# Chunked attention and a GELU layer: where the reciprocals of the first two tiles are spread, and which queue loads V

## The chip, the cores and the metric

The kernel runs on one core of a Trainium2 chip. The metric is the device time of one execution in microseconds (us); before the change it is 291.14 us, the median of three runs (290.89 to 291.3).

## The reference, cut to what matters

```python
B, H, S, D = 8, 8, 576, 64            # q, k, v: float32
q_c = q.reshape(B, H, 9, 64, D)       # chunks of 64 queries, of 64 keys
scores = np.matmul(q_c, k_c.transpose(0, 1, 2, 4, 3)) / np.sqrt(D)
attn = np.exp(scores - scores.max(-1, keepdims=True))
attn = attn / (attn.sum(-1, keepdims=True) + 1e-09)
x = np.matmul(attn, v_c)              # -> 4608 tokens x 512 (heads side by side)
h = x @ w_in                          # 512 -> 2048
y = gelu(h) @ w_out                   # 2048 -> 512, exact GELU; float32 out
```

Each chunk of 64 tokens attends to itself alone, so the softmax is over 64 keys. The kernel leaves the maximum out (the scores are small) and divides after the product with V: x = (P V) times the reciprocal of P's sums.

## The kernel before

**Tiles.** The 4608 tokens are cut into nine tiles of 512. Tiles 0 to 7 are the first eight chunks of one batch; tile 8 holds the ninth chunk of all eight batches. For each tile, attention makes x (128 partitions of model dimension x 4 groups `g` x 512 tokens; a group is a pair of heads), `mm1` makes h (16 slices `f` of 128 hidden units, four products of 128x128 with 128x512 each, then a GELU on ScalarE), and `mm2` makes y (four blocks `ms` of 128 tokens, sixteen products each). TensorE's products are bf16 into float32 PSUM banks.

**PSUM.** Eight banks: three of the tag "mm", two "tp", three "at". A tile that asks for a bank of a tag waits until one is free.

**Order.** The whole program is written out by hand (`manual_schedule`): every engine works through its instructions in the order in which the program issues them. While a tile's `mm1` and `mm2` run (`phase`), the attention of the next tile is put between the products: `extra2` names what goes ahead of which step of `mm2`. SyncE's queue (SP) issues nearly all transfers, in order.

**The first tile** has nothing to hide behind. For each group: cast q (VectorE) and k (POOL), transpose them on TensorE (`att_T`, copied out by VectorE for q and ScalarE for k), scores (`att_S`), exp on ScalarE, then `att_av`: P's columns are the stationary operand and V with a column of ones (`v_one`) moves, so that av lies with queries on partitions and its 65th column holds the sums. VectorE takes the reciprocals (line 329) and multiplies (line 331; for one half of group 2 ScalarE does so, line 335), `att_x` transposes the result back on TensorE (line 340) and a copy puts it into x (line 341). `keep_warm` puts products without use between these, and `mm1_first` starts the first two f group by group, as x comes (line 360). From f = 2 on, `mm1_slot` follows (line 371).

**The second tile's attention** lies inside tile 0's `mm2`, which runs by rows there: step s takes f = s for all four ms (`mm2_rows`, line 447), so that w_out is needed only as it arrives. At steps 3 to 8 q and k are transposed, at 9 the scores come (`quad_S`), at 11 the column sums by products with ones (`column_sums`, line 216), a 32x32-block transpose and a reciprocal on VectorE (lines 220, 222). `over` then moves the reciprocals between partitions with 16 small ScalarE copies (line 227), `spread` makes four 128x512 tiles of them by broadcasting transposes (line 231). At 12 come the product with V (`quad_av`, line 275) and the multiplication into x (`quad_x`, line 283). After steps 0 to 13, `mm2_last` adds the last two f to each ms (line 429), `rows_out` copies y out, and `mm1_first(1, ...)` makes four f of tile 1. Only then `phase(1)` goes on with line 371. Later tiles get their reciprocals in another way (`quad_total`, `quad_rc`), which stays.

**Loads.** SP issues, in order: q, k, V of tile 0 mixed with w_in's four quarters; then w_out's first quarter, tile 1's q, w_out's second, tile 1's k, w_out's third, tile 1's V (nine transfers of rows of 256 bytes, `rows_128` at line 105: four for even heads, five for odd ones), w_out's last quarter in two halves, and tile 2's q and k. All go through seven staging buffers of 1 MB and are cast to bf16 by POOL, VectorE or (one slice of w_out) ScalarE.

Of the kernel before, what the change touches and what calls it, by code (L numbers as in the profile page):

```python
# [11 lines left out]
def kernel(  # L12
# [9 lines left out]
    nc = tc.nc  # L22
# [28 lines left out]
    v_one = consts.tile([P, H, CT // 2, D + 2], bf16, name="v_one")  # L51
    nc.gpsimd.memset(v_one[:, :, :, D:D + 1], 1.0)
# [49 lines left out]
    def rows_128(t, src, raw, swapped, parity=range(2)):  # L102

        def go(to, rows):
            nc.sync.dma_start(to, rows.rearrange("h key d -> key h d"))
        last = CT // 2 - 1
        if t < B and not swapped:
            for n in range(CT // 2):
                go(raw[:, :, n], src[t, :, P * n:P * (n + 1), :])
        elif t < B and 0 in parity:  # L110
            for n in range(CT // 2):
                go(raw[:, 0::2, n], src[t, 0::2, P * n:P * (n + 1), :])
# [16 lines left out]
    def load_v_rows(t, parity=range(2)):  # L129
        if "vf" not in tiles[t]:  # L130
            tiles[t]["vf"] = stage_tile()[:].rearrange("p (h n d) -> p h n d", h=H, d=D)
        rows_128(t, v, tiles[t]["vf"], True, parity)

    def load_v(t, heads):

        if "vf" not in tiles[t]:
            tiles[t]["vf"] = stage_tile()[:].rearrange("p (h n d) -> p h n d", h=H, d=D)
        for h in heads:
            nc.sync.dma_start(tiles[t]["vf"][:, h], v[t, h, 0:MT, :].rearrange("(n key) d -> key n d", key=P))
# [8 lines left out]
    def cast_v(t, g, copy):  # L148
        copy(v_one[:, 2 * g:2 * g + 2, :, 0:D], tiles[t]["vf"][:, 2 * g:2 * g + 2])
# [62 lines left out]
    def column_sums(t):  # L212
# [10 lines left out]
        rb = work.tile([P, G, NB], f32, tag="rb1", name="rb1", bufs=1)  # L223

        def over(m):
            for s in range(G):
                nc.scalar.copy(rb[QD * s:QD * (s + 1), m], r1[QD * m:QD * (m + 1), s // 2])  # L227

        def spread(m):
            rc = work.tile([P, NB, 32], f32, tag="rc", name="rc", bufs=4)  # L230
            nc.vector.transpose(rc[:], rb[:, m].to_broadcast([P, NB, 32]))
            tiles[t]["rc", m] = rc
        return over, spread
# [79 lines left out]
    def att_av(t, g, banks, second=None):  # L313
# [3 lines left out]
        av = [pool.tile([P, half, D + 1], f32, tag=tag, name="av_ps") for pool, tag in banks]  # L317
        for n in range(half):
            for r in range(2):
                for c in range(2):  # L320
                    cs = slice(CH * c, CH * (c + 1))
                    nc.tensor.matmul(av[r][cs, n, :], st["pT", 2 * (g // 2) + r][cs, half * (g % 2) + n, :],
                                     v_one[cs, 2 * g + r, n, 0:D + 1], start=True, stop=True,
                                     tile_position=(CH * c, CH * c))
        xn = work.tile([P, half, 2, D], bf16, tag="xn", name="xn", bufs=4)
        st["xn", g] = xn
        rr = work.tile([P, 2, half, 1], f32, tag="rr", name="rr", bufs=4)
        for r in range(2):
            nc.vector.reciprocal(rr[:, r], av[r][:, :, D:D + 1])
            if r == 0 or second is None:  # L330
                nc.vector.tensor_tensor(xn[:, :, r], av[r][:, :, 0:D], rr[:, r].to_broadcast([P, half, D]),
                                        op=mybir.AluOpType.mult)
            else:
                for n in range(half):
                    nc.scalar.activation(xn[:, n, r], av[r][:, n, 0:D], Act.Copy, scale=rr[:, r, n])

    def att_x(t, g, copy, pool, tag):
        tp = pool.tile([P, CT // 2, P], bf16, tag=tag, name="tp")
        for n in range(CT // 2):
            nc.tensor.transpose(tp[:, n], tiles[t]["xn", g][:, n].rearrange("p r d -> p (r d)"), ident[:])  # L340
# [332 lines left out]
```

## Time and profile before

| | |
|---|---|
| median of the runs | 291.14 us (290.89 to 291.3) |
| the profiled execution | 290.1 us |
| its span (first to last instruction) | 288.3 us |
| TensorE busy | 277.9 us, 96% |
| ScalarE, VectorE, POOL busy | 60%, 36%, 25% |
| granted TensorE clock | full |
| moved by DMA | 53.87 MB, 187 GB/s over the span |
| end of the first attention (first `mm1_slot`) | 20.43 us |
| column sums of tile 1 | 44.66 us |
| first `mm1_slot` of tile 1 | 55.62 us |

All of it is one profiled execution, times counted from the span's start. A line such as L371 is a line of the kernel. Each row names the engine (PE is TensorE, DVE VectorE, ACT ScalarE, SP SyncE), the operation, its output and inputs by the program's names and the shape. Rows of the timeline join instructions that follow one another closely; matmuls overlap, so a group's time includes the tail of its last one. What stands in brackets is how long the engine had been idle before the row, and what ended that.

### The profile page before, as it was taken

How to read it: one execution, taken by the hardware profiler on the slowest of the kernel's cores; microseconds unless marked ns; L12 is line 12 of the kernel's file. 1: busy time of each engine (PE TensorE's matmuls, PEld its weight loads, DVE VectorE, ACT ScalarE, POOL GpSimd, SP SyncE). 2: the span in 40 equal slices, each digit the busy share in tenths (PEclk: the TensorE clock that was granted, in tenths of full speed). 3: DMA queues.
4: the chain of work that ended last, by engine and by line, in shares of the span. 5: the costliest groups of instructions: out<-in, count | busy, mean ns of one | idle time of the engine just before them, and what ended most of it. 6: DMA issues, size and time to landing. Idle time of an engine off the chain costs nothing.

```text
span 288.3 us, 5998 instructions
## 1 busy us (share of the span) xinstructions
PE 277.9 (96%) x2427; PEld 132.2 (46%) x2427; DVE 104.5 (36%) x201; ACT 174.2 (60%) x364; POOL 72.4 (25%) x121
## 2 busy tenths in 40 slices
PE   7689997999999999999999999999999999999994
PEld 3344453444444444444444444444444444444443
DVE  2744235304910391039202920293029301940021
ACT  3567749677646873777367736863786368637400
POOL 3545673611620620052015200620024110000000
PEclk9999999999999999999999999999999999999999
DMA  7999989799899926991699159834995590030033
GB/s 230 307 372 382 400 215 342 170 267 246 201 278 279 221 81 187 270 219 55 178 287 210 58 165 265 199 103 151 190 159 117 156 217 2 19 129 0 0 75 73
DMA packets 118939, 53.87 MB, mean 187 GB/s; under 512 B 97792, under 2 KB 111360, under 8 KB 118912
## 3 DMA queue, kind: packets, MB, share of 16 engines
q1 hardware_dynamic: 118752, 53.36, 70.8%
q8 instruction: 19, 0.31, 0.5%
q10 hardware_dynamic: 160, 0.13, 0.2%
q14 instruction: 8, 0.07, 0.1%
HBM read 36.70 MB, written 9.44 MB: 160 GB/s over the span
## 4 chain that ended last, share of the span: by engine, by line
PE 93%; ACT 2%; DVE 2%; DMA 1%; issue 0%; POOL 0%; SPq 0%; POOLq 0%
PE h_ps L371 41%; PE y_ps L386 38%; PE y_ps L447 3%; PE h_ps L360 2%; PE av_ps L275 2%; PE s_ps L196 2%; PE tp L155 1%; PE y_ps L415 1%; ACT rb L227 1%; DMA arrival<-in_k_dram 1%; PE warm L505 1%; PE y_ps L429 1%; ACT x L341 1%; PE tp L340 0%; DVE qT L157 0%; DVE q_nat L146 0%
## 5 line engine op out<-in xcount | busy, mean ns | idle before, releaser
L371 PE MATMUL h_ps<-x,w_in_sb 128*128 128x512 bf16 x552 | 120.6, 379 | 0.0
L373 ACT ACTIVATE h<-h_ps 128x512 bf16<-128x512 f32 x138 | 82.3, 598 | 60.1 <-PE h_ps L371 60.1
L386 PE MATMUL y_ps<-w_out_sb,h 128*128 128x512 bf16 x496 | 109.7, 379 | 0.0
L371 PEld LDWEIGHTS <-w_in_sb 128*128 128x128 bf16 x552 | 54.0, 98 | 65.2
L386 PEld LDWEIGHTS <-h 128*128 128x128 bf16 x496 | 47.4, 98 | 55.8
L241 DVE STREAM_TRANSPOSE pt<-pT 128x256 f32<-128x256 f32 x28 | 12.2, 437 | 110.4 <-ACT pT L207 110.4
L146 POOL CAST q_nat<-arrival 128x512 bf16<-128x512 f32 x31 | 18.0, 621 | 97.1 <-DMA arrival<-in_q_dram 94.6
L169 POOL CAST v_nat<-arrival 128x1024 bf16<-128x1024 f32 (+1 forms) x18 | 16.8, 945 | 40.3 <-DMA arrival<-in_v_dram 40.3
L510 ACT ACT_TABLE_LOAD x18 | 23.1, 1283 | 1.0 <-PEq L657 0.7
L254 ACT COPY part<-part 32x32 f32<-32x32 f32 x56 | 12.2, 219 | 15.1 <-DVE part L244 14.6
L287 DVE TENSOR_TENSOR x<-av_ps,rc 128x512 bf16<-128x512 f32 x28 | 18.9, 676 | 2.2
L244 DVE TENSOR_REDUCE part<-pt 128x16 f32<-128x512 bf16 x28 | 19.2, 686 | 1.0
L400 DVE COPY y_sb<-y_ps 128x512 f32<-128x512 f32 x10 | 6.9, 692 | 34.8 <-PE y_ps L386 34.8
L144 POOL CAST k_nat<-arrival 128x512 bf16<-128x512 f32 x28 | 16.2, 614 | 0.9 <-DMA arrival<-in_k_dram 0.9
L400 ACT COPY y_sb<-y_ps 128x512 f32<-128x512 f32 x25 | 14.2, 583 | 1.5 <-PE y_ps L429 0.7
L447 PE MATMUL y_ps<-w_out_sb,h 128*128 128x512 bf16 x56 | 13.6, 379 | 1.4 <-POOL w_out_sb L494 1.4
L207 ACT ACTIVATE pT<-s_ps 128x512 bf16<-128x512 f32 x28 | 14.3, 594 | 0.0
L505 PE MATMUL warm<-rest 128*128 128x512 bf16 x23 | 8.5, 460 | 1.7 <-DVE rest L47 1.2
L268 DVE STREAM_TRANSPOSE rc<-rb 128x512 f32<-128x512 f32 x14 | 9.9, 707 | 0.2
L268 DVE STREAM_TRANSPOSE rc<-across 128x512 f32<-128x512 f32 x14 | 9.8, 700 | 0.0
L494 POOL CAST w_out_sb<-arrival 128x512 bf16<-128x512 f32 x11 | 7.3, 693 | 6.2 <-DMA arrival<-in_moe_w_out_dram 6.1
L484 POOL CAST w_in_sb<-arrival 128x512 bf16<-128x512 f32 x10 | 6.8, 702 | 5.7 <-DMA arrival<-in_moe_w_in_dram 5.7
(66 smaller groups left out, 137.9 us busy)
## 6 DMA issues: line engine op xcount, KB each, us to landing
out_dram<-y_sb SPq DMA_DIRECT2D x32, 256.0 KB, 2.1
arrival<-in_v_dram SPq DMA_DIRECT2D x57, 128.0 KB, 3.9
arrival<-in_k_dram SPq DMA_DIRECT2D x28, 256.0 KB, 6.0
arrival<-in_q_dram SPq DMA_DIRECT2D x7, 1024.0 KB, 6.6
arrival<-in_moe_w_out_dram SPq DMA_DIRECT2D x3, 1024.0 KB, 12.8
arrival<-in_moe_w_in_dram SPq DMA_DIRECT2D x4, 512.0 KB, 5.5
arrival<-in_moe_w_in_dram SPq DMA_DIRECT2D x2, 1024.0 KB, 8.7
arrival<-in_v_dram SPq DMA_DIRECT2D x30, 64.0 KB, 2.6
```

Of the source, the lines that this page charges most:

```text
L144: copy(st[nm][:, :, g], st[nm + "f"][:, :, g].rearrange("p (q r) d -> p q r d", r=2))
L146: copy(st[nm][:, g].rearrange("p j r d -> p r j d"), st[nm + "f"][:, 2 * g:2 * g + 2])
L169: copy(st["v"][:, r::2, ns], st["vf"][:, r::2, ns])
L244: nc.vector.tensor_reduce(st["part", g2][:, c, :, :, 0], pt[:].rearrange("p n e u -> p n u e"), axis=mybir.AxisListType.X, op=mybir.AluOpT ...
L268: nc.vector.transpose(rc[:], tiles[t]["rb", g2][c].to_broadcast([P, NB, 32]))
L287: nc.vector.tensor_tensor(x.rearrange("p n (e u) -> p n e u", u=2), st["av"][g2][c][:].rearrange("p n (e u) -> p n e u", u=2), st["rc", 2 ...
L371: nc.tensor.matmul(h_ps[:], w_in_sb[:, ks, f * P:(f + 1) * P], st["x"][:, ks, :], start=(ks == 0), stop=(ks == KS - 1))
L373: nc.scalar.activation(st["h"][:, f, :], h_ps[:], Act.Gelu)
L386: nc.tensor.matmul(y_ps[:], st["h"][:, f, ms * P:(ms + 1) * P], w_out_sb[:, f, :], start=(f == 0), stop=(f == FF - 1))
L400: (AC if t == 0 or ms < 3 and t + 1 < NT else DV)(y_sb[:], y_ps[:])
L447: nc.tensor.matmul(tiles[t]["y_ps", ms][:], tiles[t]["h"][:, fi, ms * P:(ms + 1) * P], w_out_sb[:, fi, :], start=(fi == 0), stop=False)
L510: nc.scalar.activation(act_scratch[:, 0:1], rest[:, 0:1], func)
```

## The change

For the first tile, the sums no longer come with the product. `att_sums` makes them on TensorE from P and a matrix of two columns of ones and takes their reciprocals; `att_spread` multiplies these, each repeated over 64 columns, with a float32 matrix of ones and zeros (`ident_f`), so that the reciprocals of a pair of heads come out along the free dimension on all partitions, and ScalarE copies the bank to SBUF. `att_av` now has V as the stationary operand and P moving: d lies on partitions, as x needs it, and VectorE's multiplication writes x itself. `att_x` and `v_one` are gone.

For the second tile, `over` does its moves as eight float32 products of `ident_f` with the reciprocals, into a bank of the tag "at", from which the four transposes read. The last two f of tile 0's `mm2` (`mm2_last`) stand inside `mm1_first(1, ...)`, which makes two f instead of four.

V's even heads for tile 1 are issued from ScalarE's queue, one transfer each ahead of f = 4, 6, 8 and 10 of tile 0's `mm1`; its odd heads stay on SP. POOL casts the first piece of V between slices of w_out. The fourth slice of w_in's first quarter is cast by VectorE instead of POOL.

```diff
-    v_one = consts.tile([P, H, CT // 2, D + 2], bf16, name="v_one")
-    nc.gpsimd.memset(v_one[:, :, :, D:D + 1], 1.0)
+    ident_f = consts.tile([P, G, 2, QD], f32, name="ident_f")
+    for r in range(2):
+        nc.gpsimd.tensor_copy(ident_f[:, :, r], ident[:].rearrange("p (g e) -> p g e", e=QD))
+    ones_r = consts.tile([P, 64], bf16, name="ones_r")
+    nc.gpsimd.memset(ones_r[:], 0.0)
+    for c in range(2):
+        nc.gpsimd.memset(ones_r[CH * c:CH * (c + 1), c:c + 1], 1.0)
...
-        rb = work.tile([P, G, NB], f32, tag="rb1", name="rb1", bufs=1)
-        def over(m):
-            for s in range(G):
-                nc.scalar.copy(rb[QD * s:QD * (s + 1), m], r1[QD * m:QD * (m + 1), s // 2])
-        def spread(m):
-            rc = work.tile([P, NB, 32], f32, tag="rc", name="rc", bufs=4)
-            nc.vector.transpose(rc[:], rb[:, m].to_broadcast([P, NB, 32]))
-            tiles[t]["rc", m] = rc
+        def over():
+            rb = ps_at.tile([P, G, NB], f32, tag="at", name="rb_ps")
+            for m in range(G):
+                for r in range(2):
+                    nc.tensor.matmul(rb[CH * r:CH * (r + 1), m], ident_f[:, m].rearrange("p r e -> p (r e)"), r1[:, r],
+                                     start=True, stop=True, tile_position=(0, CH * r))
+            for m in range(G):
+                rc = work.tile([P, NB, 32], f32, tag="rc", name="rc", bufs=4)
+                nc.vector.transpose(rc[:], rb[:, m].to_broadcast([P, NB, 32]))
+                tiles[t]["rc", m] = rc
...
+    def att_sums(t, g, pool, tag):
+        st = tiles[t]
+        half = CT // 2
+        sT = pool.tile([P, half // 2, 2, 2], f32, tag=tag, name="sT")
+        for a in range(half // 2):
+            for r in range(2):
+                u = half * (g % 2) + 2 * a
+                nc.tensor.matmul(sT[:, a, r], st["pT", 2 * (g // 2) + r][:, u:u + 2].rearrange("p u e -> p (u e)"),
+                                 ones_r[:, 0:2], start=True, stop=True)
+        st["rr", g] = work.tile([P, half // 2, 2, 2], f32, tag="rr", name="rr", bufs=4)
+        nc.vector.reciprocal(st["rr", g][:], sT[:])
+
+    def att_spread(t, g, pool, tag):
+        st = tiles[t]
+        half = CT // 2
+        rc_ps = pool.tile([P, half, 2, CH], f32, tag=tag, name="rc_ps")
+        for a in range(half // 2):
+            for c in range(2):
+                for r in range(2):
+                    nc.tensor.matmul(rc_ps[CH * r:CH * (r + 1), 2 * a:2 * a + 2, c],
+                                     st["rr", g][:, a, r, c:c + 1].to_broadcast([P, D]), ident_f[:, :, 0],
+                                     start=True, stop=True, tile_position=(0, CH * r))
+        st["rc", g] = work.tile([P, half, 2, CH], f32, tag="rc", name="rc", bufs=4)
+        nc.scalar.copy(st["rc", g][:], rc_ps[:])
+
+    def att_av(t, g, banks):
+        st = tiles[t]
+        half = CT // 2
+        av = [pool.tile([P, half, CH], f32, tag=tag, name="av_ps") for pool, tag in banks]
         for n in range(half):
             for r in range(2):
                 for c in range(2):
-                    cs = slice(CH * c, CH * (c + 1))
-                    nc.tensor.matmul(av[r][cs, n, :], st["pT", 2 * (g // 2) + r][cs, half * (g % 2) + n, :],
-                                     v_one[cs, 2 * g + r, n, 0:D + 1], start=True, stop=True,
-                                     tile_position=(CH * c, CH * c))
...
+                    cs, rs = slice(CH * c, CH * (c + 1)), slice(CH * r, CH * (r + 1))
+                    nc.tensor.matmul(av[c][rs, n], st["v"][cs, 2 * g + r, n],
+                                     st["pT", 2 * (g // 2) + r][cs, half * (g % 2) + n, :], start=True, stop=True,
+                                     tile_position=(CH * c, CH * r))
+        x = st["x"][:, g, :].rearrange("p (n c e) -> p n c e", c=2, e=CH)
+        for c in range(2):
+            nc.vector.tensor_tensor(x[:, :, c], av[c][:], st["rc", g][:, :, c], op=mybir.AluOpType.mult)
...
-        keep_warm(1)
+        att_sums(0, 0, *at)
         att_T(0, "q", 2, DV)
         att_S(0, (1,))
-        keep_warm(1)
+        att_spread(0, 0, *mm)
         cast_qk(0, "q", 3, DV)
         att_T(0, "k", 2, AC)
+        att_sums(0, 1, *at)
         att_T(0, "q", 3, DV)
-        keep_warm(1)
         att_S(0, (2,))
+        att_spread(0, 1, *mm)
         att_T(0, "k", 3, AC)
         keep_warm(1)
         att_av(0, 0, (tp, tp))
+        att_sums(0, 2, *at)
         att_S(0, (3,))
         att_av(0, 1, (at, mm))
+        att_spread(0, 2, *mm)
         keep_warm(1)
-        att_x(0, 0, AC, *mm)
-        keep_warm(2)
-        mm1_first(0, (mm, mm),
...
+        mm1_first(0, (mm, tp),
+                  (((0, 1), (0,)), lambda: att_sums(0, 3, *at), lambda: keep_warm(1), lambda: att_av(0, 2, (at, at)),
+                   ((0, 1), (1,)), lambda: att_spread(0, 3, *mm), lambda: act_table(Act.Gelu), lambda: keep_warm(1),
+                   lambda: att_av(0, 3, (at, tp)), ((0, 1), (2,)), lambda: win[0](3, DV), lambda: keep_warm(1),
                    ((0, 1), (3,))))
+        v_arrival(1)
...
-                    load_v_rows(1)
+                    load_v_rows(1, (1,))
...
+        def late_casts():
+            a, b = slice(0, 2), slice(2, 4)
+            wout[2](0, PO)
+            wout[2](1, PO)
+            cast_v_rows(1, 0, PO, a)
+            wout[2](2, PO)
+            wout[2](3, PO)
+            cast_v_rows(1, 0, PO, b)
+            cast_v_rows(1, 1, PO, a)
+            cast_v_rows(1, 1, PO, b)
+            for i in (0, 1, 3):
+                wout[3](i, PO)
...
-                  12: [lambda: quad_av(1)]
+                  11: [lambda: over.append(column_sums(1))],
+                  12: [lambda: over[0](), lambda: quad_av(1)]
                       + [lambda m=m: quad_x(1, m // 2, m % 2) for m in range(G)] + [lambda: wout[3](2, AC)]},
-              by_rows=True, first=2)
+              by_rows=True, first=2,
+              extra1={**{4 + 2 * n: [lambda n=n: load_v_rows(1, (0,), (n,), nc.scalar)] for n in range(CT // 2)},
+                      12: [late_casts]})
         pool_cast_qk(2)
-        mm1_first(1, (mm, mm, tp, at),
-                  (((0, 1), (0, 1)), lambda: rows_out(0, 2), ((2, 3), (0, 1)), lambda: rows_out(0, 3),
-                   ((0, 1, 2, 3), (2, 3))))
+        mm1_first(1, (tp, at), (((0, 1), (0, 1)), *[lambda ms=ms: mm2_last(0, ms) for ms in range(MT // P)],
+                                ((0, 1), (2, 3))))
...
-            phase(t, e2, first=4 if t == 1 else 0)
+            phase(t, e2, first=2 if t == 1 else 0)
```

## The prediction

> **What bounds the kernel now.** The page's head and the chain that ended last come first: TensorE is the bound, 93% of the chain, so anything that delays it by 1 us costs 1 us unless it was waiting there anyway.
>
> ```profile
> span 288.3 us, 5998 instructions
> ...
> PE 277.9 (96%) x2427; PEld 132.2 (46%) x2427; DVE 104.5 (36%) x201; ACT 174.2 (60%) x364; POOL 72.4 (25%) x121
> ...
> PE 93%; ACT 2%; DVE 2%; DMA 1%; issue 0%; POOL 0%; SPq 0%; POOLq 0%
> ```
>
> From 55.6 us on, the chain is TensorE alone, 29.2 us a tile, and the change ends there. So I read TensorE's timeline up to that point (start, duration, line, idle before). A duration holds about 0.17 us of tail; what an operation costs in a row is start to start.
>
> ```profile
> 8.64 0.40 PE L155 MATMUL tp<-ident,q_nat 128*128 128x128 bf16 x4 [1.09 <-DVE q_nat L146]
> ...
> 20.00 0.59 PE L360 MATMUL h_ps<-x,w_in_sb 128*128 128x512 bf16 x2
> 20.43 12.25 PE L371 MATMUL h_ps<-x,w_in_sb 128*128 128x512 bf16 x56
> ...
> 41.20 1.03 PE L447 MATMUL y_ps<-w_out_sb,h 128*128 128x512 bf16 x4
> ...
> 44.66 0.48 PE L216 MATMUL sums_ps<-pT,ones_c 128*32 128x512 bf16 x4
> 45.08 1.04 PE L447 MATMUL y_ps<-w_out_sb,h 128*128 128x512 bf16 x4
> 46.05 0.74 PE L275 MATMUL av_ps<-pT,v_nat 64*64 64x64 bf16 x64
> 48.21 1.89 PE L447 MATMUL y_ps<-w_out_sb,h 128*128 128x512 bf16 x8 [1.43 <-POOL w_out_sb L494]
> 50.45 1.89 PE L429 MATMUL y_ps<-w_out_sb,h 128*128 128x512 bf16 x8 [0.35 <-ACT w_out_sb L494]
> 52.17 3.62 PE L360 MATMUL h_ps<-x,w_in_sb 128*128 128x512 bf16 x16
> 55.62 10.52 PE L371 MATMUL h_ps<-x,w_in_sb 128*128 128x512 bf16 x48
> ```
>
> Three marks: the head (first attention) ends at 20.43; the second tile's column sums start at 44.66, call it T; that tile's first four f end at 55.62. Between T and 55.62 TensorE waits 1.78 us, for the last quarter of w_out, which VectorE's and POOL's timelines set beside the chain of the reciprocals:
>
> ```profile
> 45.18 0.72 DVE L220 STREAM_TRANSPOSE t<-sums_ps 128x512 f32<-128x512 f32 x1 [3.02 <-PE sums_ps L216]
> 45.93 0.35 DVE L222 RECIPROCAL r<-t 128x32 f32<-128x32 f32 x1
> ...
> 38.64 2.29 POOL L494 CAST w_out_sb<-arrival 128x512 bf16<-128x512 f32 x4 [0.99 <-DMA arrival<-in_moe_w_out_dram]
> ...
> 47.55 1.86 POOL L494 CAST w_out_sb<-arrival 128x512 bf16<-128x512 f32 x3 [2.80 <-DMA arrival<-in_moe_w_out_dram]
> ```
>
> Last the stretches of two us (busy times, clock, share of the DMA engines, GB/s): the loads are saturated from 2 to 38 us, and only while V's 256-byte rows come is there slack.
>
> ```profile
> 28.00:30.00 2.00, 2.00 (x11) 0.93 (x10) 1.17 (x2) 1.32 (x3) 1.61 (x2) 1.00 1.09 400
> ...
> 40.00:42.00 2.00, 2.00 (x18) 1.03 (x14) 1.22 (x2) 1.04 (x2) 2.00 (x5) 1.00 0.72 161
> ...
> 58.00:60.00 2.00, 2.00 (x11) 0.94 (x10) 0.00 (x0) 1.42 (x3) 0.00 (x0) 1.00 1.03 232
> ```
>
> The profiled execution took 290.1 us, 1.8 outside its span; the median is 291.14, so I add differences to the median. About 0.2% (0.58 us) is what a measurement of this kernel tells from no change.
>
> **Part 1, the head.** Out go, per pair of heads, four transposes (0.22 us of TensorE), ScalarE's copy of x (0.58), one of two reciprocals (0.18). In come `att_sums` (4 products, a reciprocal of 0.18) and `att_spread` (8 float32 products, then a ScalarE copy of a 128x512 bank, 0.58). V's products are as before, and VectorE's two multiplications (0.42 and, behind it, 0.34) now write x. Nothing differs until q's third cast ends and TensorE resumes, 8.62. From there TensorE's list, at start-to-start prices: 4 groups of transposes at 0.24, 3 of scores and 4 of V at 0.25, 3 of sums at 0.24 (four weight loads, as for transposes), 5 warming products at 0.22, 4 pairs of h at 0.43: 6.25 us. Call one spread X. Three waits follow spreads, whatever X: the third scores need k's copy, queued on ScalarE behind the spread's copy (0.17 tail + 0.04 + 0.49 + 0.58 + 0.04 = 1.32, against 0.72 of TensorE's work: 0.60); the fourth the same (against 0.95: 0.37); the last h needs copy and two multiplications (0.17 + 0.04 + 0.58 + 0.04 + 0.76 + 0.04 = 1.63 against 1.12: 0.51). End of the head: 8.62 + 6.25 + 1.48 + 4X = 16.35 + 4X; it is at 20.43 now, so X = 1.02 breaks even. V's last cast (15.90) and w_in's casts are earlier than their uses then.
>
> X is in no row: no float32 product runs now. Low end: 128 columns at the bf16 price of a transpose (0.055), both column halves at once: 8 x 0.055 / 2 = 0.22. High end: a float32 product made of four parts (two bf16-sized halves of each operand), so as long as 512 bf16 columns (0.216), plus a weight load of 0.098 that nothing covers: 8 x 0.314 = 2.5. The nearest row is L216: four 512-column products on four column strips took 0.42 start to start where singly they would take 0.86, so two ran at a time. With such a pairing X is 0.86, without it 1.73; I take the middle, 1.3. Head: 21.55, 1.1 us later.
>
> In the trace 64-column weight loads take 107 ns, 128-column ones 98 (L322, L371). The Trainium skill, "TensorE: Matmul & The Clock Gate", section "Weight-path perf modes", has a rule against this part behind that: float32 weights, and loads of fewer than 128 columns, get no fast weight load. By its section "LDWEIGHTS" a 64-column load is an estimated 53 ns; uncovered, eight in each of four spreads would add 1.7 us, and the total would be 295.1 instead of 293.4. No float32 row shows it, and the sum leaves it out.
>
> POOL's new work before its first cast (two copies, three memsets for one removed, some 1 us by its 0.1 to 0.3 us rows) fits in its 2.64 us of idle there; without that cover k's first cast would be late by as much. w_in's fourth slice goes from POOL to VectorE (0.6 us), in time for f = 3. The warming products left out give their places to real ones.
>
> **Part 2, half of V.** Its nine transfers stay nine, but four leave SP, where they stood ahead of w_out's last quarter, for ScalarE's queue, 2 to 7 us after the head: into the saturated stretch. At 232 GB/s (the row at 58) 0.52 MB delays what follows by 2.3 us. w_out's third quarter lands at 38.6, is cast by 39.25 and used at 41.20: slack 1.95, so T cannot come much earlier than now however fast the head; a head 1.1 us later hides it all. In return w_out's last quarter is issued behind five V transfers, not nine, and lands 1 to 3 us earlier (1 MB at 360 to 400 GB/s behind half the rows): the 1.78 us of waits go. V takes its staging buffer first, and each later load gets the buffer freed next; the fourth of w_out keeps that of w_in's fourth, cast by 26.4. POOL casts V's first piece between w_out's slices: +0.6 us for the third of these, used over 1 us later.
> Each issue also holds ScalarE's queue. SP's V issues took 0.50 to 2.03 us, median 0.61. A GELU takes 0.60 of each 0.86 us; two and a median issue make 1.81 against 1.73, a lag that three h banks absorb: 0. At 2.03 the lag is 1.5 each, 6.0 less 0.96 of slack: 5.0. I take 0, since its queue carries no other transfer, and keep 5.0.
>
> **Part 3, the second tile.** Out go 16 ScalarE copies (3.44 us, L227), in come 8 small float32 products (Y) into a third "at" bank; the four transposes of 0.71 stay. Reciprocals are there at T + 1.62; TensorE, done with its four products at T + 1.39, waits 0.27 with its own latency, then Y. Y: 64 products of V take 0.67, so at least 8 x 0.0105 = 0.08; at most eight loads of 0.107, 0.86; I take the middle, 0.45. Add 0.17: transposes start at T + 2.3 and take 3 x 0.63 + 0.71 = 2.6, to T + 4.9. The three "at" banks hold y's last rows, the sums and these products; V's second half needs the third, so TensorE stands from about T + 2.4 to T + 4.94. Behind the stop in its queue: 32 V products (0.34), 8 of w_out (1.73), then two f over half of x (0.86), eight closing w_out (1.73), the rest of the two f (0.86), two more f (1.73): T + 12.2. x's first half is multiplied by T + 6.2, no limit. Now it is T + 10.96: the 1.78 us of waits removed return as 2.8, plus Y, less 0.2 of tails that two stops fewer leave out. Cost: 1.2 us (0.9 with Y at its low end, 1.8 at its high end with transposes at 0.71).
>
> Sum: 1.1 + 0 + 1.2 = 2.3; 291.14 + 2.3 = 293.4.
>
> **Rivals.**
> A, cheap float32 (ends faster). If X is 0.5, the head ends 2.1 us earlier. For it speaks that nothing in the profile excludes it; against it L216 and the DMA share above 1.0. It decides only if the V half costs w_out less than it seems: with Y at its low end, faster by 0.58 needs T earlier by 1.5, so X at 0.65 or less and w_out's third quarter later by at most 0.5. Time: 291.14 - 2.1 + 0.9 = 289.9.
> B, dear float32: X of 2.2, serial and with half its loads bare. Head + 4.7, total 291.14 + 4.7 + 1.2 = 297.0. Against it: L216's overlap.
> C, ScalarE's queue stands in its DMA issues: 293.4 + up to 5.0, say half, 295.9. For it: SP's 2.03 us; against: its queue is empty. A worse form: SP's waits show V issues waiting for q's landing (1.7 us in 4), semaphores taken in turn; a V issue given one of w_out's would hold GELU until that landed, over 10 us.
> D, no change: V's half is hidden and the faster head is eaten by part 3, X near 0.7: 291.14 - 1.3 + 1.2 = 291.0.
>
> **How the numbers follow.** Forecast (X 0.9 to 1.75) 0.52, own range 291.9 to 295.3; A 0.13, B 0.14, C 0.12 (0.02 its worse form), D 0.09. Range 289.9 (A) to 297.0 (B). Leaving out half of A, half of B and a quarter of C is 0.17. Faster: A and 0.04 of D, 0.17; same: the rest of D and the low edge of the forecast, 0.10; slower 0.73.
>
> **What would show it.** `att_spread` start to start near 1.3 and the first L371 near 21.5; sums near 45.8; w_out's last cast no longer waited for; TensorE idle about 2.5 us inside V's products; first L371 of the second tile, two f in, near 56.2. Wrong if spreads take under 0.7, if V's products don't stop, or if GELUs stop behind ScalarE's issues.

## The result and the profile after

The changed kernel takes 299.25 us (median of four runs, 298.6 to 299.99) against 291.01 (290.58 to 291.3): a ratio of 1.0285, 95% interval 1.0251 to 1.0318. It is 8.2 us slower. The forecast was 293.4 with a range up to 297.0: the right side, but the time is outside the range. The profiled execution took 299.8 us, 9.7 more than that of before, and the marks below account for these 9.7.

First the head of the page and of the chain that ended last, and the costliest group (columns: line, engine, operation, count | busy us, mean ns | idle us before, and what ended most of it):

```profile
span 298.0 us, 6101 instructions
...
PE 280.6 (94%) x2470; PEld 135.3 (45%) x2499; DVE 103.0 (35%) x198; ACT 170.3 (57%) x345; POOL 73.1 (25%) x124
...
PE 88%; DMA 7%; issue 1%; ACT 1%; DVE 1%; SPq 0%; POOL 0%; ACTq 0%
...
L394 PE MATMUL h_ps<-x,w_in_sb 128*128 128x512 bf16 x551 | 123.5, 382 | 5.6 <-ACT h L396 5.2
```

TensorE has fallen from 93% of the chain to 88%, and 7% now belong to DMA, 5% of them to a load of q. The products of h, which before waited for nothing, stand 5.2 us for ScalarE. TensorE's timeline of the changed kernel shows where (start, duration, line, idle before and what ended it):

```profile
9.01 1.09 PE L344 MATMUL rc_ps<-ident_f,rr 128*64 128x128 f32 x16
10.03 0.40 PE L164 MATMUL tp<-ident,k_nat 128*128 128x128 bf16 x4
...
20.74 4.48 PE L394 MATMUL h_ps<-x,w_in_sb 128*128 128x512 bf16 x20
27.11 3.61 PE L394 MATMUL h_ps<-x,w_in_sb 128*128 128x512 bf16 x16 [1.89 <-ACT h L396]
34.00 5.81 PE L394 MATMUL h_ps<-x,w_in_sb 128*128 128x512 bf16 x19 [3.28 <-ACT h L396]
39.65 2.75 PE L469 MATMUL y_ps<-w_out_sb,h 128*128 128x512 bf16 x12
...
51.80 0.48 PE L225 MATMUL sums_ps<-pT,ones_c 128*32 128x512 bf16 x4
...
53.57 0.64 PE L237 MATMUL rb_ps<-r,ident_f 128*64 128x16 f32 x16 [0.32 <-DVE r L231]
54.15 0.47 PE L285 MATMUL av_ps<-pT,v_nat 64*64 64x64 bf16 x34
56.82 0.44 PE L285 MATMUL av_ps<-pT,v_nat 64*64 64x64 bf16 x30 [2.20 <-DVE rc L241]
...
64.06 2.11 PE L394 MATMUL h_ps<-x,w_in_sb 128*128 128x512 bf16 x9
```

Mark by mark, in us:

| stretch | before | after | difference |
|---|---|---|---|
| start to first `mm1_slot` of tile 0 (end of the head) | 20.43 | 20.74 | +0.31 |
| from there to the first product of `mm2` | 12.08 | 18.91 | +6.83 |
| from there to the column sums (T) | 12.15 | 12.15 | 0 |
| T to the slot of f = 4 of tile 1 | 10.96 | 13.99 | +3.03 |
| from there to the end of the span | | | -0.5 |

(The last row of the timeline starts at f = 2; two slots of 0.86 put f = 4 at 65.79.) The head's 0.31 is no measure of part 1: where the head is the old one, it ended at 20.57, 21.09 and 21.49 in other profiled executions, and the new one between 20.24 and 23.08. The loop of h holds two stops, 1.89 and 3.28; 1.66 of its loss is left over. In the second tile 1.2 is what the forecast summed; 1.8 is left over. The two leftovers have one cause, which the stretches of 3.41 us show (columns: stretch, length, busy us and count of PE, weight loads, DVE, ACT, POOL; then granted clock, DMA share, GB/s):

```profile
29.92:33.33 3.41, 0.80 (x4) 0.29 (x3) 1.17 (x3) 0.00 (x0) 1.60 (x3) 1.00 1.11 384
33.33:36.74 3.41, 2.74 (x7) 0.99 (x7) 1.05 (x3) 2.17 (x4) 2.60 (x5) 0.50 1.09 382
...
53.81:57.22 3.41, 1.21 (x79) 1.03 (x77) 2.97 (x5) 0.07 (x1) 3.33 (x6) 1.00 0.74 166
57.22:60.63 3.41, 3.19 (x14) 1.18 (x10) 1.91 (x4) 0.00 (x0) 1.29 (x3) 0.50 1.00 205
```

Behind the second stop of the loop, and behind the one inside V's products, TensorE ran 3.41 us at half clock: 1.7 us lost each time, with the engine "busy". The profiled execution of the kernel before has full clock throughout this part. So 5.17 us of stops, 3.4 of clock, 1.3 of the second tile's new order and 0.3 of the head make 10.2, less 0.5 at the end.

Why the loop of h stops is read from ScalarE's timeline in the changed kernel (ACTq rows are issues of transfers):

```profile
22.66 0.60 ACT L396 ACTIVATE h<-h_ps 128x512 bf16<-128x512 f32 x1 [0.25 <-PE h_ps L394]
25.98 0.43 ACTq L110 DMA_DIRECT2D arrival<-in_v_dram  x1
26.46 0.60 ACT L396 ACTIVATE h<-h_ps 128x512 bf16<-128x512 f32 x1 [3.20 <-POOL w_in_sb L506]
26.51 0.47 ACTq L110 DMA_DIRECT2D arrival<-in_v_dram  x1
26.95 1.81 ACT L396 ACTIVATE h<-h_ps 128x512 bf16<-128x512 f32 x3
32.93 0.38 ACTq L110 DMA_DIRECT2D arrival<-in_v_dram  x1
33.35 0.60 ACT L396 ACTIVATE h<-h_ps 128x512 bf16<-128x512 f32 x1 [4.58 <-DMA arrival<-in_q_dram]
33.40 0.46 ACTq L110 DMA_DIRECT2D arrival<-in_v_dram  x1
```

The issues themselves are short here, 0.38 to 0.47 us. What they wait for is long, and ScalarE works through its queue in order, so the GELU behind an issue waits too. The first waits for its staging buffer, that of w_in's third quarter, which POOL cast until 25.94: ScalarE idle 3.20 us. POOL's timeline has the cast:

```profile
24.33 1.61 POOL L506 CAST w_in_sb<-arrival 128x512 bf16<-128x512 f32 x2 [1.88 <-DMA arrival<-in_moe_w_in_dram]
```

The third waits until tile 1's q has landed, at 32.91: idle 4.58. In the trace the transfers of both queues take eight completion semaphores in turn, and the third V issue waits for the very one that tile 1's q was given. With three h banks TensorE absorbs about 1.3 us of each wait and stands the rest.

### The profile page after: what moved, and what is told of

Its sections match the earlier page's. It is cut to its first block, busy times and chain, and to the rows that moved or that the text cites. A ratio compares the mean times of both kernels' runs of the same rounds, so it can differ in the third digit from the quotient of the medians.

```text
span 298.0 us, 6101 instructions
## 1 busy us (share of the span) xinstructions
PE 280.6 (94%) x2470; PEld 135.3 (45%) x2499; DVE 103.0 (35%) x198; ACT 170.3 (57%) x345; POOL 73.1 (25%) x124
## 4 chain that ended last, share of the span: by engine, by line
PE 88%; DMA 7%; issue 1%; ACT 1%; DVE 1%; SPq 0%; POOL 0%; ACTq 0%
PE h_ps L394 38%; PE y_ps L409 36%; DMA arrival<-in_q_dram 5%; PE y_ps L469 4%; PE av_ps L285 2%; DMA arrival<-in_k_dram 2%; PE s_ps L205 2%; PE y_ps L438 1%; PE rc_ps L344 1%; PE h_ps L383 1%; PE tp L164 1%; PE y_ps L452 1%; DVE rc L241 1%; ACT kT L166 1%; SPq L100 0%
## 5 line engine op out<-in xcount | busy, mean ns | idle before, releaser
L394 PE MATMUL h_ps<-x,w_in_sb 128*128 128x512 bf16 x551 | 123.5, 382 | 5.6 <-ACT h L396 5.2
L394 PEld LDWEIGHTS <-w_in_sb 128*128 128x128 bf16 x560 | 55.1, 98 | 72.6 <-issue 7.4
L251 DVE STREAM_TRANSPOSE pt<-pT 128x256 f32<-128x256 f32 x28 | 12.2, 437 | 114.3 <-ACT pT L216 114.3
L264 ACT COPY part<-part 32x32 f32<-32x32 f32 x56 | 12.3, 219 | 15.0 <-DVE part L254 14.6
L216 ACT ACTIVATE pT<-s_ps 128x512 bf16<-128x512 f32 x28 | 14.3, 593 | 0.0
L285 PE MATMUL av_ps<-pT,v_nat 64*64 64x64 bf16 x512 | 6.1, 194 | 2.2 <-DVE rc L241 2.2
```

The costliest lines, as they stand in the source:

```text
L394: nc.tensor.matmul(h_ps[:], w_in_sb[:, ks, f * P:(f + 1) * P], st["x"][:, ks, :], start=(ks == 0), stop=(ks == KS - 1))
```

## The experiments

The theory after the result: part 1 costs nothing; part 2 costs by what the V issues wait for; part 3 costs by the bank that the transposes hold; and each long stop brings a stretch of half clock. The rivals: the price of an issue on ScalarE's queue, the traffic, and the float32 products.

**V's nine transfers back on SP** (the rest of the change kept).

```
-                    load_v_rows(1, (1,))
+                    load_v_rows(1)
...
-              extra1={**{4 + 2 * n: [lambda n=n: load_v_rows(1, (0,), (n,), nc.scalar)] for n in range(CT // 2)},
-                      12: [late_casts]})
+              extra1={12: [late_casts]})
```

> The changed kernel with all nine of V's transfers back on SP, in their old place; head and second tile as changed. Theory (ScalarE's queue stood in V's issues for 5.2 us, and the half clock that followed took 1.7 more): GELUs of tile 0 run without a stop, first L394 to the first product of mm2 takes 12.1 us as before the change, 18.9 with it; total 292.6 if the stop inside V's products leaves the clock alone, 294.3 if the clock still halves there. Rival (the head or the second tile's products cost most of the 8.2 us): stays above 296.

Measured: 293.18 us, ratio 1.0072 (1.0039 to 1.0105). The loop of h took 12.08 us as before, without a stop. The 2.20 us stop in V's products of the second tile stayed. The runs spread from 291.4 to 295.3; the profiled one (295.24) had two stretches of 3.41 us at half clock one after the other there, from 50.19. So six of the 8.2 us are V's half on ScalarE's queue.

The granted clock of the ten executions sorts them: 291.4 and 291.8 us at 1.000, five of 293.0 to 293.3 us at 0.992 to 0.994, three of 294.7 to 295.3 us at 0.983 to 0.987. One stretch of 3.41 us at half clock lowers the mean over 293 us by 0.006, so the groups fit no such stretch, one and two, at some 1.7 us each. Both numbers of the theory, 292.6 and 294.3, lie between groups of executions.

**Each part alone, on the kernel before.** V's half on ScalarE's queue:

```
...
+        v_arrival(1)
...
-                    load_v_rows(1)
+                    load_v_rows(1, (1,))
...
+              extra1={**{4 + 2 * n: [lambda n=n: load_v_rows(1, (0,), (n,), nc.scalar)] for n in range(CT // 2)},
+                      12: [late_casts]})
```

> The kernel before with V's even heads on ScalarE's queue ahead of f = 4, 6, 8, 10, and POOL's casts in the changed order, nothing else. Theory: the third issue waits for the landing of tile 1's q near 31 us, GELU stands, TensorE stops for 3 to 4 us and its clock halves for 3.4 us; against that the wait for w_out's last quarter (1.8 us) goes: total 294 to 297. Rival (V's half is harmless, the stop comes of the head's new timing): 289 to 291.5.

The second tile's reciprocals by products, with `mm2_last` inside `mm1_first`:

```
...
-        rb = work.tile([P, G, NB], f32, tag="rb1", name="rb1", bufs=1)
...
+        def over():
+            rb = ps_at.tile([P, G, NB], f32, tag="at", name="rb_ps")
...
-        mm1_first(1, (mm, mm, tp, at),
...
+        mm1_first(1, (tp, at), (((0, 1), (0, 1)), *[lambda ms=ms: mm2_last(0, ms) for ms in range(MT // P)],
+                                ((0, 1), (2, 3))))
```

> The kernel before with the second tile's part alone: reciprocals moved by float32 products into an at bank, mm2's last two f inside mm1_first. Theory: TensorE stands 2.2 us inside V's products until the four transposes have left the bank; cost 1.3 us with a full clock, 292.4, and 3.0 with the clock halved behind the stop, 294.1. Rival (the waits for w_out are gone only because everything was late, so nothing is lost): 291.

The first tile's new attention (V's staging buffer is taken first here too, as in the changed kernel):

```
-    def att_x(t, g, copy, pool, tag):
...
+    def att_sums(t, g, pool, tag):
...
+    def att_spread(t, g, pool, tag):
...
```

> The kernel before with the head alone: sums and spreads of tile 0 on TensorE, V stationary. Theory: a spread takes 1.02 us, the head ends 0.3 us later, 291.4. Rival (the shorter chain of the last group is worth more once V's transfers leave ScalarE alone): head 0.5 us earlier or more, 290.5.

Measured: V's half 297.82 us, ratio 1.0211 (1.0172 to 1.025); the second tile's part 293.98, 1.0099 (1.0065 to 1.0134); the head 290.49, 0.9971 (0.9943 to 0.9998). The three ratios add to +2.8%, the whole change is +2.85%: within the intervals the parts add up. V's half alone shows stops of 0.31 and 4.15 us in the loop of h and one half-clock stretch. It is 0.8 us above the theory's range, which took the wait for w_out's last quarter as gone; TensorE's timeline of this kernel still has it:

```profile
57.99 1.89 PE L430 MATMUL y_ps<-w_out_sb,h 128*128 128x512 bf16 x8 [1.84 <-ACT w_out_sb L497]
```

The second tile's part alone has the 2.20 us stop and one half-clock stretch, as expected. The head is no loss, by the median 0.5 us of gain, at the edge of what can be told from none. That is the rival's number and not the theory's 291.4, but its reason, a head that ends earlier, isn't shown: in the profiled execution, the slowest of the ten, the head ended at 20.93.

**One more staging buffer**, to take the first of the two waits away and leave the second.

```
-    stage = ctx.enter_context(tc.tile_pool(name="stage", bufs=7))
+    stage = ctx.enter_context(tc.tile_pool(name="stage", bufs=8))
```

> The changed kernel (299.25 us) with eight staging buffers instead of seven, nothing else. V's first transfer then gets a buffer whose casts end about 2 us sooner; the third transfer still waits for the semaphore of tile 1's q, which lands at 32.9 us. Theory (two waits of their own kind, one after the other): the stop of 1.89 us at f = 7 goes, the second one stays and grows by what was gained, since q's landing does not follow the loop of h; the half clock behind it stays; 297.0 to 299.3 us. Rival (the buffer's wait is the whole cause and the second stop only its echo): both stops and the half clock go, 292 to 293.5 us.

Measured: 301.05 us, 1.0357 (1.031 to 1.0404). The two rows, from ScalarE's and from TensorE's timeline of this kernel:

```profile
33.72 0.60 ACT L396 ACTIVATE h<-h_ps 128x512 bf16<-128x512 f32 x1 [6.82 <-DMA arrival<-in_q_dram]
```

```profile
34.37 6.00 PE L394 MATMUL h_ps<-x,w_in_sb 128*128 128x512 bf16 x20 [5.51 <-ACT h L396]
```

The first issue went at 22.99 without a wait and the first stop is gone, but all of it came back in the second: 5.51 us, where 1.89 and 3.28 had been. The loop ran up to the GELU behind the third issue and stood there for q, wherever it had been before. The rival, one wait and its echo, falls. The time is 1.75 us above the theory's range. Two of the four executions show a granted clock of 0.981, where the changed kernel shows 0.989 to 0.992; the rest of the excess is not explained.

**Two of the four transfers**: the third and fourth go on SP.

```
-                    load_v_rows(1, (1,))
+                    load_v_rows(1, ns=(2, 3))
...
-              extra1={**{4 + 2 * n: [lambda n=n: load_v_rows(1, (0,), (n,), nc.scalar)] for n in range(CT // 2)},
+              extra1={**{4 + 2 * n: [lambda n=n: load_v_rows(1, (0,), (n,), nc.scalar)] for n in range(2)},
```

> The changed kernel with only the first two of V's even transfers on ScalarE's queue (ahead of f = 4 and 6); the third, which waited for q's semaphore, and the fourth go on SP before the five odd ones. Theory (the second stop is the semaphore): the stop of 1.89 us stays, that of 3.28 us and the half clock behind it go; 299.25 - 3.28 - 1.7 = 294.3 us, 293.3 to 295.3. Rival (any transfer in that queue holds ScalarE, or the traffic moves the loss): 297 us or more.

Measured: 295.99 us, 1.0173 (1.0138 to 1.0207). TensorE's timeline of this kernel:

```profile
27.65 7.93 PE L394 MATMUL h_ps<-x,w_in_sb 128*128 128x512 bf16 x36 [1.79 <-ACT h L396]
```

The loop of h has this one stop, behind the buffer's wait, and full clock, and takes 14.04 us instead of 18.91. That is the 4.9 us expected, though the median fell by 3.3 only and lies 0.7 above the theory's range; in the profiled pair 0.6 of the difference is a head that ended later.

**All four together, but ahead of the last GELU**, where buffer and semaphores are free. POOL now casts all of w_out's third quarter ahead of V.

```
...
-              extra1={**{4 + 2 * n: [lambda n=n: load_v_rows(1, (0,), (n,), nc.scalar)] for n in range(CT // 2)},
-                      12: [late_casts]})
+              extra1={15: [lambda: load_v_rows(1, (0,), queue=nc.scalar), late_casts]})
```

> The changed kernel with V's four even transfers still on ScalarE's queue, but issued ahead of the GELU of the last f instead of ahead of f = 4, 6, 8 and 10, so that the semaphores and the buffer they need have long been free; POOL casts w_out's third quarter before V. Theory (the loss of part 2 is what the issues wait for, not the queue or its time per issue): h of the first tile runs without the stops of 1.89 and 3.28 us and without the half clock behind them: 299.25 - 5.2 - 1.7 = 292.4, 291.5 to 293.5 us. Rival (ScalarE's queue or the traffic itself costs): 295 us or more.

Measured: 297.11 us, 1.0219 (1.0171 to 1.0268). The theory's number fell. The loop of h did run in 12.09 us, but the stop came one step later. ScalarE's and TensorE's timelines of this kernel:

```profile
32.56 3.87 ACTq L110 DMA_DIRECT2D arrival<-in_v_dram  x4
36.48 0.60 ACT L396 ACTIVATE h<-h_ps 128x512 bf16<-128x512 f32 x1 [3.46 <-DVE w_out_sb L516]
```

```profile
33.08 1.46 PE L469 MATMUL y_ps<-w_out_sb,h 128*128 128x512 bf16 x6
37.12 1.58 PE L469 MATMUL y_ps<-w_out_sb,h 128*128 128x512 bf16 x6 [2.59 <-ACT h L396]
```

Issued in a row the four held ScalarE for 3.87 us, the last one alone for 2.27. The GELU of the last f waited behind them, `mm2`'s next rows needed the bank that it empties, TensorE stood 2.59 us, and 3.41 us at half clock followed. So the price of an issue is real as well when the queue is pressed: 0.4 us each when spread out (once 1.44, with V's half alone), 2 us for the fourth of a burst. The rival that prices the issue holds to this extent.

The same move on the kernel with the first part alone, as a candidate for a better version:

```
...
-                    load_v_rows(1)
+                    load_v_rows(1, (1,))
...
+              extra1={15: [lambda: load_v_rows(1, (0,), queue=nc.scalar), late_casts]})
```

> Before with part 1 (head_alone, 290.49 us) and V's four even transfers on ScalarE's queue ahead of the GELU of the last f; the second tile's reciprocals as before. Theory: w_out's last quarter is issued behind five V transfers instead of nine, lands 1 to 2 us earlier, and the wait for it of 2.09 us goes or falls under 0.8: 288.6 to 289.7 us, faster than both kernels. Rival: V's even rows land later than now (their casts are POOL's last before w_out's last slices), V's products wait about as long as w_out's did: 290.3 to 291.5 us.

Measured: 294.7 us, 1.012 (1.0074 to 1.0167), above both numbers expected, by the same stop (2.21 us) and a half-clock stretch behind it; a wait of 1.84 us near the end of `mm2` stayed too, now for ScalarE's cast of w_out.

**The bank of the second tile**, on the kernel with V on SP: ScalarE copies the eight products' bank, the transposes read the copy.

```
+            rb_sb = work.tile([P, G, NB], f32, tag="rb1", name="rb1", bufs=1)
+            nc.scalar.copy(rb_sb[:], rb[:])
...
...
-                nc.vector.transpose(rc[:], rb[:, m].to_broadcast([P, NB, 32]))
+                nc.vector.transpose(rc[:], rb_sb[:, m].to_broadcast([P, NB, 32]))
```

> The changed kernel with V's nine transfers on SP (v_on_sp, 293.18 us) and one thing more: ScalarE copies the eight products' bank to SBUF (about 0.3 us), and the four transposes read the copy, so the third bank of V's products is free some 2 us sooner. Theory (the 2.20 us stop in V's products is the bank held by the transposes, and the stop brings the half clock): the stop shrinks to 0.3 to 0.8 us, no half-clock stretch follows near 50 us, about 1.5 us of waiting for x come in its place behind the first products of w_out; 290.5 to 291.7 us. Rival 1 (the stop has another cause): 2.2 us stay, 293 to 293.5. Rival 2 (bank right, but the half clock comes for another reason): the stop shrinks and the 3.41 us at half clock stay, 292.3 to 293.

Measured: 291.08 us, 1.0018 (0.9996 to 1.0039). TensorE's timeline of this kernel:

```profile
49.66 0.81 PE L287 MATMUL av_ps<-pT,v_nat 64*64 64x64 bf16 x64
50.40 1.90 PE L471 MATMUL y_ps<-w_out_sb,h 128*128 128x512 bf16 x8
53.73 1.02 PE L385 MATMUL h_ps<-x,w_in_sb 128*128 128x512 bf16 x4 [1.43 <-DVE x L295]
```

All 64 products of V run through, the wait for x of 1.43 us comes in the stop's place, and the clock stays full behind it. The bank was the stop's cause. (The profiled execution, 292.89 us, is the slowest of the ten; its head ended at 23.08.)

**The clock by itself**, on the same kernel with V on SP: eight products of zeros, added to an open row of y, run in the stop. They change nothing in y and release no bank.

```
...
+            if t == 1 and i == 34:
+                for _ in range(8):
+                    nc.tensor.matmul(tiles[0]["y_ps", 3][:], rest[:, 0:P], rest[:], start=False, stop=False)
...
```

> v_on_sp (293.18 us) with eight 128x512 products of zeros, added into the open rows of y (1.73 us of work without use), put in TensorE's queue where V's products stop for 2.20 us. Nothing else is touched, V's second half is not released any earlier. Theory (the half clock follows from the stop itself, TensorE having too little work in one 3.41 us window): the idle time falls to about 0.5 us, the clock stays full, and 1.7 to 2 us come back although useless work was added: 290.8 to 291.7 us. Rival (the clock falls there for another reason, such as what the products are): 3.41 us at half clock stay, 293.0 to 293.7.

Measured: 292.1 us, 1.0042 (1.0024 to 1.006), 1.1 less than without the useless products. TensorE's timeline of this kernel:

```profile
48.64 1.90 PE L287 MATMUL y_ps<-rest 128*128 128x512 bf16 x8
50.91 0.44 PE L288 MATMUL av_ps<-pT,v_nat 64*64 64x64 bf16 x30 [0.37 <-DVE rc L241]
```

V's second half still comes when the transposes release the bank; only the emptiness of the stop is gone, and with it the half clock. From T to f = 4 it is 12.3 us, against 15.1 in the profiled execution without them, which ran twice 3.41 us at half clock. Of the six executions five show a granted clock of 0.997 to 1.000, of the ten without the products only two did. That the half clock follows from the stop is shown. By the medians the gain is below the theory's 1.7 to 2, for the products cost something too: the two executions that kept their clock without them took 291.4 and 291.8 us.

**The three mends at once**: eight buffers, two of the four transfers, the bank copied.

```
-    stage = ctx.enter_context(tc.tile_pool(name="stage", bufs=7))
+    stage = ctx.enter_context(tc.tile_pool(name="stage", bufs=8))
...
+            nc.scalar.copy(rb_sb[:], rb[:])
...
-                    load_v_rows(1, (1,))
+                    load_v_rows(1, ns=(2, 3))
...
```

> The three mends together: the changed kernel with two of the four V transfers left on ScalarE's queue, eight staging buffers, and the products' bank copied to SBUF by ScalarE. Theory (buffer, semaphore and bank are the whole loss, with the half clocks that follow them): no stop of TensorE over 0.5 us while h of the first tile runs, at most 0.8 us in V's products, some 1.4 us of waiting for x, no half clock before the end; 289.8 to 291.2 us. Rival (V's early rows delay w_out and k by their traffic): a stop of 1 to 3 us at k or w_out's third quarter, 292 to 294.5 us.

Measured: 291.41 us, 1.0026 (1.0007 to 1.0044). No stop in the loop of h, none in V's products, full clock to the end; 0.75 us for w_out's third quarter and the 1.43 us for x remain. Of the 2.85% lost 2.6% are back: buffer, semaphore, bank and the clock behind them are the loss, but for 0.26%. The time is 0.2 us above the range expected.

**Towards a better version.** The first part with eight buffers:

```
-    stage = ctx.enter_context(tc.tile_pool(name="stage", bufs=7))
+    stage = ctx.enter_context(tc.tile_pool(name="stage", bufs=8))
```

> Part 1 alone (head_alone, 290.49 us) with eight staging buffers. Theory: w_out's last quarter and the loads ahead of it are issued sooner, the stop of 2.09 us for its casts shrinks below 1 us and the half clock that followed it does not come; 288.4 to 289.7 us, faster than both kernels. Rival (the loads are bound by the transfers themselves, not by buffers): the stop stays, 290.1 to 290.8 us.

Measured: 290.15 us, 0.9984 (0.9957 to 1.001): not to be told from before, and in the rival's range. The clock stayed full in the profiled run, but a wait of 1.83 us near the end of `mm2` remained, and not for the landing. ScalarE's and TensorE's timelines of this kernel:

```profile
46.13 3.44 ACT L236 COPY rb<-r 32x16 f32<-32x16 f32 x16
49.59 0.62 ACT L516 CAST w_out_sb<-arrival 128x512 bf16<-128x512 f32 x1
```

```profile
50.26 1.89 PE L451 MATMUL y_ps<-w_out_sb,h 128*128 128x512 bf16 x8 [1.83 <-ACT w_out_sb L516]
```

All of w_out had landed by 47.17; its slice on ScalarE waited behind the 16 copies of reciprocals. So that cast goes to POOL, in this kernel, in the one with seven buffers, and in the kernel before:

```
-        for i in (0, 1, 3):
+        for i in range(4):
             wout[3](i, PO)
...
-                      + [lambda m=m: quad_x(1, m // 2, m % 2) for m in range(G)] + [lambda: wout[3](2, AC)]},
+                      + [lambda m=m: quad_x(1, m // 2, m % 2) for m in range(G)]},
```

> head_eight_buffers (290.15 us) with the third slice of w_out's last quarter cast by POOL, behind its other three, instead of by ScalarE behind the 16 copies of reciprocals. Theory (the wait of 1.83 us is ScalarE's queue: its copies ran from 46.13 to 49.59 and the cast behind them, while all of the quarter had landed by 47.17): POOL's cast ends near 48.5, TensorE's wait falls from 1.83 to 0.3 us or less, 288.3 to 288.9 us, faster than both kernels. Rival (the quarter's landing is the wait): 1.3 us or more stay, 289.7 to 290.5.

> The same cast moved to POOL in head_alone (290.49 us, seven buffers). There the quarter landed 1.5 us later against the column sums, and TensorE stood 2.09 us for POOL's first slice. Theory (two limits one behind the other, landing first): the wait stays at 1.3 to 2.1 us in the profile, 290.0 to 290.5 us. Rival (ScalarE's queue alone): the wait goes below 0.5, 288.5 to 289.2 us.

> The kernel before with only this cast moved from ScalarE to POOL. Its waits were 1.43 us for POOL's cast (the landing) and 0.35 us for ScalarE's. Theory: the 0.35 us go, or less since POOL's last cast comes 0.5 us later, the 1.43 stay: 290.4 to 291.0 us beside 290.9. Rival: both go, 289.1 to 289.5.

Measured: 290.0 us, 0.9978 (0.996 to 0.9996); 289.93, 0.9963 (0.9941 to 0.9985); 290.67, 0.9993 (0.9977 to 1.0009). The wait for ScalarE's cast is gone in all three, but no run gained the full 1.8 us, and the first missed the theory's 288.3 to 288.9: with eight buffers V's last rows landed at 46.92 this time and the quarter's first half at 48.10, not 45.71, so TensorE waited 0.60 and 0.36 us for them. In the kernel before with this cast on POOL, the wait for POOL's first slice is 1.22 us. With the first part and seven buffers it is 1.17 us:

```profile
48.57 1.89 PE L469 MATMUL y_ps<-w_out_sb,h 128*128 128x512 bf16 x7 [1.17 <-POOL w_out_sb L516]
```

Both limits exist, the landing and ScalarE's queue, one behind the other. The first part with the cast on POOL, 289.93 us, is, with the one of eight buffers at 290.0, the fastest version found: 0.37% below the kernel before and 3.1% below the changed one. The eighth buffer adds nothing that can be told.

## Why the prediction was wrong, point by point

**Part 1, +1.1 us: the term X was too large.** Alone the part cost nothing (0.9971). A spread takes 1.02 us from start to start (9.01 to 10.03), not 1.3, and 1.02 is just the break-even that the formula gives. Each float32 product is two passes in the trace, each with a weight load of 136 ns; 16 loads on two column halves are 8 x 0.136 = 1.09, so by this estimate the loads alone fill the time. The paired reading of L216 (0.86) was nearer than the middle taken. From the resume at 8.26 in this run the formula gives 20.07; the head ended at 20.74, 0.67 later, with 0.48 of it a wait of V's products for exp's result (14.59), which the list of waits lacks.

By the Trainium skill, "TensorE: Matmul & The Clock Gate", section "Weight-path perf modes", float32 weights get no fast load; the prediction had worked out 1.7 us extra from it. The loads are in fact longer here, 136 ns for 64 columns, where 53 had been estimated and 128 columns of bf16 take 98, but the head as a whole was no slower alone.

**Part 2, 0 us taken: the step that failed.** The runs showed stops of 5.17 us in its place and 1.7 us of half clock behind them. Two of its sentences were wrong. "V takes its staging buffer first, and each later load gets the buffer freed next": V got the buffer of w_in's third quarter and waited for POOL until 25.98. "I take 0, since its queue carries no other transfer": the issue's length is not what counts; the semaphores are shared with SP's transfers, so an empty queue does not help. The prediction's own last sign of being wrong, GELUs that stop behind ScalarE's issues, is what came. The right mechanism stood under rival C as its "worse form", at 0.02, with w_out in the place of q and over 10 us in the place of 4.58. It deserved far more, since SP's row of V issues waiting for q's landing was in the profile before. With the two stops measured, 5.2 us, the sum would have been 298.6. What the part was to give back came otherwise: w_out's last quarter landed at 46.88 and 48.25, not 1 to 3 us earlier but 0.5 to 0.6. Its waits went because T was 7.1 us later and because the 16 copies were gone from ScalarE's queue: with V's half alone T was 7.5 us later, and TensorE still waited 1.84 us for ScalarE's cast behind the copies. The traffic's price, w_out's third quarter landing later, was hidden behind the stops (42.00 instead of 38.59); with the stops mended it shows as 0.75 us, against 0.34 with all of V on SP.

**Part 3, +1.2 us: right, but for what it brings.** The products took 0.58 (Y was 0.45), the stop lasted 2.20 us up to T + 5.02 (forecast T + 4.94), and without the half clock f = 4 would have come at T + 12.3 (forecast 12.2). Missing is the 1.7 us of clock behind the stop. Alone, the part cost 1.0%, with that stretch in it.

**The clock was in no step and in no rival.** It makes 3.4 of the 9.7 us in the profiled pair. The profile before gave no row of half clock there. Its waits were 1.78 us in two pieces, which may be why, but the kernel before was not far from it either, as the last section shows.

## What to carry to other kernels

A transfer that is moved to another engine's queue takes its waits along: before pricing the issue, find what buffer and which completion semaphore it will wait for, and what stands behind it in that in-order queue. A stop of TensorE of about 2 us can cost a stretch at half clock on top of its own length, here 1.7 us in most executions (eight of ten with V on SP): split it or fill it where that can be done. When a wait is removed, look for the next one at the same place (here ScalarE's cast behind the landing, and q's semaphore behind the buffer) before counting the gain.

## What the hardware showed that was not expected

The half clock comes in stretches of 3.41 us or twice that, and the two in the changed kernel start 23.89 us apart, seven times 3.41: the stretches lie on a fixed grid. What TensorE did in the grid's window before a stretch goes with it. In all eleven windows of these profiles, ahead of the last products, with 0.00 to 1.27 us of busy TensorE the next was at half clock; in ten with 1.5 to 2.0 it was not. One of the ten is the kernel before, around its wait for w_out:

```profile
46.69:50.10 3.41, 1.98 (x16) 0.87 (x9) 2.45 (x4) 3.19 (x16) 1.79 (x3) 1.00 1.11 338
```

Two windows with 1.76 and 1.91 us busy, in part with transposes and 64x64 products, were followed by half clock all the same, so the busy time alone does not settle it; what else counts stays open. The Trainium skill, "TensorE: Matmul & The Clock Gate", Part 1, gives a free-running window of 3413 ns, which agrees, and throttling after at least one idle window of that length, which does not, if idle means without work: here a stop of 2.09 us (the first part alone) was enough, in a window with 1.27 us of work.

Where a stop falls in the grid differs from execution to execution, and the granted clock on record fits that. Of twenty executions of the kernel before, measured beside the first experiments, fifteen show 0.997 or more and took 290.0 to 291.3 us; five show 0.988 to 0.994 and took 292.1 to 293.2. The same sorting, in the kernel with V on SP, gave the groups above. So a stop near 2 us costs its stretch in some executions and not in others, and a difference of one stretch between two profiles need not be one between two kernels.
